# Passage to attention: the third unit's Q and K requested behind the first relayout, squares ahead of copies, and the halves of the first load run one after the other

## The chip, the cores and the metric

One core of one Trainium2 chip runs the whole kernel. The metric is device time in microseconds (us) for one execution, and the number compared is the median of several executions. The core's engines are named as in its profile: PE is TensorE (matrix multiply; PEld are its weight loads), DVE is VectorE, ACT is ScalarE, POOL is GpSimd and SP is SyncE, which here only issues DMA transfers. Each engine executes its own instructions strictly in program order; engines wait for each other, and for DMA transfers, by semaphores.

## What is computed

A linear recurrence in the style of attention, followed by two mixture-of-experts layers. Only the first part is touched by the change:

```python
mag = np.sqrt(a_re * a_re + a_im * a_im)
scale = np.minimum(mag, 0.999) / (mag + 1e-06)
a_re_n, a_im_n = (a_re * scale, a_im * scale)
for t in range(S):                       # S = 768, per batch (4), head (8), D = 48
    S_re, S_im = a[t] * (S_re, S_im)     # complex product, row by row
    S_re += k[:, :, t] (outer) v[:, :, t]
    y[:, :, t] = q[:, :, t] @ S_re
x = moe(y); x = moe2(x)                  # 3072 tokens, 8 experts each
```

The output is the result of the second expert layer, 3072 x 384 floats.

## The kernel before

The time axis is cut into chunks of 128 steps, 24 chunks over the 4 batches; two neighbouring chunks of a batch make a *unit*, 12 units in all. Three stages follow each other.

**The scan** (`prefix`). For all chunks at once the running products P of the normalized decays are formed, from the middle of a chunk outwards, 63 steps of two DVE instructions each: `t` (line 404, the four partial products) and `P` (line 409, their sums). The decays arrive as 16 loads `raw` of 8 steps (line 212, 215, requested by SP), and each load has two *halves* of 4 rows, so each half feeds two steps of the scan. Before a half can feed the scan, its magnitude is worked out: squares, their sum `u`, `mg` = exp(ln/2), `r` = 1/(mg + eps), `L` = r squared, `Aa`. For loads 2 to 15 this is `approx`, mostly on ACT with sums by PE into PSUM. For loads 0 and 1, when nothing else has begun, it is `approx_half`, with the sums on DVE; before the change the two halves of a load run in lockstep (`approx_halves`: every instruction comes twice, once for each half). A DVE routine `norm(j)` (five instructions) then makes the normalized decays `n` of half j, and ACT copies a negated part (line 340). The order in which all these stand is set by generators that are advanced by hand between the steps of the scan: `pull` advances the norms, `HV`, `AH`, `H0` and `H1` say how far the others go.

**The passage**. Behind the scan, the first units are prepared: `prod(n)` turns P and the loaded Q and K of unit n (tile `xy`, line 497; buffers for two units) into the tile `X`. It begins with two `squares` of P on ACT (line 542), an instruction on DVE (line 567), two on ACT (lines 568, 569), and then DVE products (line 565) and corrections (lines 575, 577, 579). When `X` of a unit is complete, `relayout` moves six pieces of it across partitions by DMA, three requested by POOL and three by SP (line 518), and `stack` makes a further copy `qst` (line 526). Units 0 and 1 are prepared completely before the attention loop; `chunk_ends` meanwhile makes the decay over a whole chunk with PE (`e_ps`), copies it on ACT (`e_sb`, line 456), writes it to DRAM (`pd`, line 457) and reads it back broadcast (`pb`, line 509).

**The attention loop**, 24 iterations, one chunk each: `scores` (PE, line 632), `masks` (DVE, line 636, product `sm` with the triangle), `kv`, `decay` (DVE, lines 673 to 677), `rows`, `store`. Between them DVE takes the pieces of `prod` for the unit two ahead. `scores(i + 1)` writes two PSUM tiles, which it can have once `masks(i)` has read them. The unit after the next is requested by `loads`: unit 2 and unit 3 ahead of the loop, the others inside it.

These lines of the passage are the ones that the change and the prediction speak of:

```python
        emit(first)                 # last pieces of prod(0), then relayout(0)
        loads_pb(0, nc.sync)
        ...
        emit(fill)                  # last pieces of prod(1), then relayout(1)
        loads(2)                    # POOL: Q and K of unit 2
        stack(U[0], SP)
        loads_pb(1, nc.sync)
        stack(U[1], SP)
        loads(3, nc.sync)           # SP: Q and K of unit 3
        scores(0, range(3, 4))
```

Of the kernel before, what the change touches and what calls it, by code (L numbers as in the profile page):

```python
# [9 lines left out]
F32 = mybir.dt.float32  # L10
# [3 lines left out]
ALU = mybir.AluOpType  # L14
# [16 lines left out]
G = B * (S // C) * 3  # L31
# [20 lines left out]
EARLY_FAST = 19  # L52
W0,W1,W2=(4, 5, 16)
LB,LA=(2, 1)
H0,H1=(6, 2)
HV=2
AH = 2
LEAD = 3
KP, SP = (3, 4, 5), ()
# [33 lines left out]
def emit(g):  # L93
    if g is not None:
        for _ in g:
            pass
# [89 lines left out]
def prefix(nc, tc, k, extra):  # L186
# [8 lines left out]
    with ExitStack() as c1:  # L195
# [55 lines left out]

        def buffers():
            return [wp.tile([128, 2, H, G], F32, name=nm, tag=nm, bufs=b)
                    for nm, b in (("mg", 1), ("L", 3), ("r0", 3), ("Aa", 3))]

        def rest(mg, L, r0, Aa):
            nc.scalar.activation(out=L, in_=mg, func=AF.Ln, bias=k.eps[:, 0:1])
# [7 lines left out]

        def approx(i):

            sq = wp.tile([128, 2, H, 2, G], F32, name="sq", tag="sq")
            nc.scalar.activation(out=sq.rearrange("p h t r g -> p (h t) r g"), in_=raw[i], func=AF.Square)  # L269
            mg, L, r0, Aa = buffers()  # L270
            yield

            def squares(x, last):
                for h in range(2):
                    for r in range(2):
                        nc.tensor.matmul(x[:, h, 0:n], k.idn, sq[:, h, :, r], start=r == 0, stop=last and r == 1)  # L276

            def view(x):
                return x[:, :, 0:n].rearrange("p h (t g) -> p h t g", g=G)

            m2 = mp.tile([128, 2, 512], F32, name="m2", tag="m2", bufs=1)
            squares(m2, True)
            for _ in range(2 if i < 4 else 4):
                yield
            nc.scalar.activation(out=L, in_=view(m2), func=AF.Ln, bias=k.tiny[:, 0:1])
            yield
            nc.scalar.activation(out=mg, in_=L, func=AF.Exp, scale=0.5)
            u = mp.tile([128, 2, 512], F32, name="u", tag="u", bufs=2)
            squares(u, False)
            for h in range(2):  # L290
                nc.tensor.matmul(u[:, h, 0:n], ide, mg[:, h], start=False, stop=True)
            pre[i] = view(u), L, r0, Aa
            yield
            yield
            yield from rest(mg, L, r0, Aa)

        def approx_half(i, h):

            if h == 0:
                u = mp.tile([128, 2, 512], F32, name="u", tag="u", bufs=2)  # L300
                sqs[i] = wp.tile([128, 2, H, 2, G], F32, name="sq", tag="sq")
                mgs[i], *lra = buffers()
                pre[i] = (u[:, :, 0:n].rearrange("p h (t g) -> p h t g", g=G), *lra)
            u, L, r0, Aa = (x[:, h] for x in pre[i])
            sq, mg = sqs[i][:, h], mgs[i][:, h]
            nc.scalar.activation(out=sq, in_=raw[i][:, h * H:h * H + H], func=AF.Square)
            yield
            nc.vector.tensor_tensor(u, sq[:, :, 0], sq[:, :, 1], op=ALU.add)
            nc.scalar.activation(out=L, in_=u, func=AF.Ln, bias=k.tiny[:, 0:1])
            yield  # L310
            nc.scalar.activation(out=mg, in_=L, func=AF.Exp, scale=0.5)
            yield
            nc.vector.scalar_tensor_tensor(out=u, in0=mg, scalar=2e-6, in1=u, op0=ALU.mult, op1=ALU.add)
            yield from rest(mg, L, r0, Aa)

        def approx_halves(i):
            for _ in zip(approx_half(i, 0), approx_half(i, 1)):
                yield

        def norm(j):  # L320

# [22 lines left out]

        load(0)
        load(1)
        firsts, halves = approx_halves(0), approx_halves(1)
        emit(islice(firsts, H0))
        emit(islice(halves, H1))
        emit(firsts)  # L350
        emit(norm(0))
        norms = chain(*(norm(j) for j in range(1, 2 * NP)))
        done = 0

# [6 lines left out]
        load(2)  # L361
        side = iter(())
        ahead = [approx(2)]
        load(3)
        routed = iter(())
        for i in range(NP):
# [10 lines left out]
            for h in range(2):  # L377
                j = 2 * i + h
                if h:
                    load(i + 4)  # L380
                    if i + 3 < NP:
                        ahead.append(approx(i + 3))
                cur = n3.pop(j)
                for ss in range(H2):
                    s = j * H2 + ss
                    a = cur[:, ss]
                    next(routed, None)
                    def more():
                        if s > 0:
                            for x in ahead:  # L390
                                for _ in range(AH):
                                    next(x, None)

                    if s == 0:
                        nc.vector.tensor_copy(P.a0, a[:, :, 0:G])
                        nc.vector.tensor_copy(P.t[:, 0, :, 1], a[:, 1:3, G:W])
                        more()
                        continue

                    if i == 0:  # L400
                        more()
                    t1 = tp.tile([128, 2, 2, W], F32, name="t1", tag="t1")
                    pairs = bass.AP(a.tensor, a.offset, [a.ap[0], [W, 2], [W, 2], [1, W]])
                    nc.vector.tensor_tensor(  # L404
                        t1, P.at(s - 1)[:, ::-1].unsqueeze(2).to_broadcast([128, 2, 2, W]), pairs, op=ALU.mult)
                    for _ in range(2 * HV):
                        next(halves, None)
                    pull(5 * j + min(LEAD, j) + (2 if ss == 0 else 4))
                    nc.vector.tensor_tensor(P.at(s), t1[:, 0], t1[:, 1], op=ALU.add)  # L409
                    pull(5 * j + min(LEAD, j) + (3 if ss == 0 else 5))  # L410
                    next(routed, None)
                    if ss:
                        next(side, None)
                    more()
        emit(side)


def chunk_ends(nc, k, psA, ep, wk):
# [35 lines left out]
    yield  # L454
    for par in range(2):
        nc.scalar.activation(out=e_sb[:, par], in_=e_ps[par].rearrange("n a r d -> n (a r d)"), func=AF.Copy)
    nc.sync.dma_start(out=k.pd, in_=e_sb)
    yield

    e2 = ep.tile([128, 2, 2 * G], F32, name="e2", bufs=1)  # L460
# [16 lines left out]
def attention(nc, tc, k, early, split):  # L477

    P = k.P
    with ExitStack() as c0:  # L480
# [123 lines left out]
        wk = c0.enter_context(tc.tile_pool(name="wk", bufs=2))  # L604
        lgb = psA.tile([128, 512], F32, name="lgb")
        wps = psA.tile([112, 4, 2, 48], F32, name="wps")
        nc.vector.memset(lgb[:, 0:128], 0.0)

        def ktr(i, rs):

# [139 lines left out]
        for _ in range(4):  # L750
            next(first)
            next(ends)
        emit(islice(first, FIRST - 4))
        next(ends)
        emit(islice(first, 4))
        squares(1, 1)
        emit(first)
        loads_pb(0, nc.sync)
        fill = prod(1, [(0, HC)])
        ktr(0, (0,))  # L760
# [18 lines left out]
        next(fill)  # L779
        ktr(0, (1,))  # L780
        emit(islice(fill, 2))
        kv(0)
        ktr(1, (0,))
        emit(fill)
        loads(2)
        stack(U[0], SP)
        loads_pb(1, nc.sync)
        stack(U[1], SP)
        loads(3, nc.sync)
        scores(0, range(3, 4))  # L790
        ktr(1, (1,))
        emit(masks(0))
        emit(decay(0))
        fill = iter(())
        for i in range(ni):
# [1276 lines left out]
```

## Time and profile before

| what | value |
|---|---|
| median of 3 runs | 694.84 us (692.77 to 696.39) |
| the profiled execution, its own time | 693.17 us |
| its span in the trace | 691.5 us |
| PE busy | 602.0 us, 87% |
| DVE busy | 567.3 us, 82% |
| ACT busy | 424.9 us, 61% |
| POOL busy | 214.9 us, 31% |

The span is what the trace shows from the first to the last instruction; the profiled execution took 1.7 us more than its span, and is itself 1.7 us quicker than the median of the runs. A busy share is an average over stages that have different limits, so what an edit is worth has to be read in its own stage. Times in the trace are counted from the start of the span.

### The profile page before, as it was taken

How to read it: one execution, taken by the hardware profiler on the slowest of the kernel's cores; microseconds unless marked ns; L12 is line 12 of the kernel's file. 1: busy time of each engine (PE TensorE's matmuls, PEld its weight loads, DVE VectorE, ACT ScalarE, POOL GpSimd, SP SyncE). 2: the span in 40 equal slices, each digit the busy share in tenths (PEclk: the TensorE clock that was granted, in tenths of full speed). 3: DMA queues.
4: the chain of work that ended last, by engine and by line, in shares of the span. 5: the costliest groups of instructions: out<-in, count | busy, mean ns of one | idle time of the engine just before them, and what ended most of it. 6: DMA issues, size and time to landing. Idle time of an engine off the chain costs nothing.

```text
span 691.5 us, 13765 instructions
## 1 busy us (share of the span) xinstructions
PE 602.0 (87%) x5024; PEld 524.1 (76%) x5024; DVE 567.3 (82%) x1218; ACT 424.9 (61%) x821; POOL 214.9 (31%) x300
## 2 busy tenths in 40 slices
PE   0799896327999999989988999999999998899996
PEld 0455564225788888878787999999999996678986
DVE  4999999986989989999799765666766677879993
ACT  6868886535457656553652655665655666478882
POOL 6400000001224332225344634444554452531101
PEclk9999999858899999999999999999999999999999
DMA  7889955006897889758350211551111168278840
GB/s 181 268 258 320 322 182 183 1 4 158 210 250 207 231 220 231 209 147 281 122 197 12 69 41 47 221 214 43 45 39 44 47 244 327 105 284 315 324 164 13
DMA packets 52167, 117.19 MB, mean 169 GB/s; under 512 B 11436, under 2 KB 40602, under 8 KB 47740
## 3 DMA queue, kind: packets, MB, share of 16 engines
q1 hardware_dynamic: 34524, 66.38, 30.9%
q0 software_dynamic: 14688, 45.94, 21.1%
q10 hardware_dynamic: 2880, 3.93, 1.8%
q8 instruction: 40, 0.66, 0.4%
q14 instruction: 35, 0.29, 0.1%
HBM read 116.84 MB, written 16.52 MB: 193 GB/s over the span
## 4 chain that ended last, share of the span: by engine, by line
PE 28%; DVE 9%; DMA 7%; issue 7%; ACT 2%; POOL 2%; POOLq 0%; ACTq 0%; DVEq 0%
PE yps L1522 11%; PE hps L1475 9%; DMA out_dram<-z,idx 3%; DMA out_dram<-y,idx 2%; DVE wlo L150 2%; DVE w L150 2%; PE gps L1351 1%; PE yps L1371 1%; DMA xg<-x,idx 1%; PE sc L632 1%; PE xtp L1459 1%; ACT w L149 1%; DVE hl L1482 1%; PE hps L1351 1%; PE yp L706 0%
## 5 line engine op out<-in xcount | busy, mean ns | idle before, releaser
L150 DVE TENSOR_TENSOR wlo<-wraw,whi 128x768 fp32r<-128x768 f32 (+1 forms) x95 | 82.3, 903 | 9.6 <-ACT whi L149 8.6
L150 DVE TENSOR_TENSOR w<-P,w 128x768 fp32r<-128x768 f32 (+1 forms) x95 | 82.6, 904 | 8.3 <-ACT w L149 7.1
L1482 DVE SCALAR_TENSOR_TENSOR hl<-hps,hh 128x512 fp32r<-128x512 f32 x48 | 33.1, 689 | 50.6 <-ACT hh L1481 47.6
L149 ACT ACTIVATE whi<-wraw 128x768 fp32r<-128x768 f32 (+1 forms) x95 | 71.0, 803 | 0.0
L149 ACT ACTIVATE w<-P 128x768 fp32r<-128x768 f32 (+1 forms) x95 | 70.8, 801 | 0.0
L1481 ACT ACTIVATE hh<-hps 128x512 fp32r<-128x512 f32 x48 | 28.7, 599 | 64.2 <-PE hps L1475 50.4
L276 PE MATMUL m<-sq,idn 128*128 128x288 f32 x112 | 35.6, 468 | 30.4 <-ACT sq L269 30.4
L1510 POOL DMA_INDIRECT out_dram<-y,idx x26 | 30.6, 1175 | 101.1 <-ACT y L1509 91.9
L632 PE MATMUL sc<-X 48*128 48x128 f32 x768 | 56.4, 293 | 5.0 <-DVE sm L636 4.5
L632 PEld LDWEIGHTS sc<-X 48*128 48x128 f32 x768 | 50.7, 201 | 10.2 <-DVE sm L636 5.2
L276 PEld LDWEIGHTS m<-sq,idn 128*128 128x128 f32 x112 | 22.7, 212 | 41.6 <-ACT sq L269 19.4
L518 POOL DMA_DIRECT2D X<-X x36 | 17.8, 502 | 107.4 <-DVE X L565 98.8
L1522 PE MATMUL yps<-w,hh 128*128 128x394 f32 x192 | 50.9, 346 | 0.0
L404 DVE TENSOR_TENSOR t<-P,n 128x576 f32<-128x576 f32 x63 | 47.5, 755 | 0.2
L1475 PE MATMUL hps<-xh,w 128*128 128x256 f32 x288 | 43.8, 282 | 3.4 <-DVE hl L1482 2.0
L1475 PEld LDWEIGHTS hps<-xh,w 128*128 128x128 f32 x288 | 38.1, 188 | 4.3 <-DVE hl L1482 2.4
L636 DVE TENSOR_TENSOR sm<-sc,tri 128x512 f32<-128x512 f32 x48 | 32.2, 684 | 8.4 <-PE sc L632 8.4
L436 POOL MEMSET ends<- 128x6 f32 x1 | 0.1, 105 | 121.6 <-DVE P L409 121.6
L704 PE MATMUL yp<-sm,v 128*64 128x128 f32 (+1 forms) x384 | 36.0, 275 | 0.0
L1522 PEld LDWEIGHTS yps<-w,hh 128*128 128x128 f32 x192 | 34.9, 189 | 0.0
L1522 PE MATMUL yps<-whi,hh 128*128 128x394 f32 x96 | 33.5, 349 | 0.0
L706 PE MATMUL yp<-qst,Ssb 96*48 96x128 f32 (+1 forms) x320 | 33.0, 282 | 0.0
(391 smaller groups left out, 1754.7 us busy)
## 6 DMA issues: line engine op xcount, KB each, us to landing
P<-in_w2t_dram SPq DMA_DIRECT2D x8, 1536.0 KB, 7.4
P<-in_v_dram SPq DMA_DIRECT2D x8, 1536.0 KB
wraw<-in_v_dram SPq DMA_DIRECT2D x8, 1536.0 KB, 7.5
qst<-X SPq DMA_DIRECT2D x48, 192.0 KB, 6.8
raw<-in_a_dram SPq DMA_DIRECT2D x32, 144.0 KB, 3.1
raw<-in_a_dram SPq DMA_DIRECT2D x64, 72.0 KB, 3.0
v<-in_v_dram POOLq DMA_DIRECT2D x12, 384.0 KB
out_dram<-xg SPq DMA_DIRECT2D x12, 384.0 KB, 3.7
```

The source lines that it names most:

```text
L149: self.nc.scalar.activation(out=hi, in_=r, func=AF.Copy)
L150: self.nc.vector.tensor_tensor(lo, r, hi.bitcast(F32), op=ALU.subtract)
L276: nc.tensor.matmul(x[:, h, 0:n], k.idn, sq[:, h, :, r], start=r == 0, stop=last and r == 1)
L404: nc.vector.tensor_tensor(t1, P.at(s - 1)[:, ::-1].unsqueeze(2).to_broadcast([128, 2, 2, W]), pairs, op=ALU.mult)
L632: nc.tensor.matmul(ps[:, pair], kk, q, start=r == 0, stop=r == 1)
L636: nc.vector.tensor_tensor(X[i].sm[:, 4 * g:4 * g + 4], X[i].sc[g], k.mask.to_broadcast([128, 4, 128]), op=ALU.mult)
L704: nc.tensor.matmul(o, U[n].v[:, c, h * 48:h * 48 + M], x.sm[:, 4 * par + pair], start=zero, stop=True)
L706: nc.tensor.matmul(o, x.sb[:, pair, 64 * par:64 * par + M], U[n].qst[:, h, cs], start=True, stop=False)
L1475: nc.tensor.matmul(ps[:, i], self.W.w1(s, wp_, j)[:, f * 128:f * 128 + 128], x[xp_][:, j], start=n == 0, stop=n == 8)
L1482: nc.vector.scalar_tensor_tensor(out=hl, in0=ps, scalar=0.0, in1=hh.bitcast(F32), op0=ALU.max, op1=ALU.subtract)
L1510: nc.gpsimd.indirect_dma_start(out=k.out, out_offset=IDX(ap=R.idx[:, c:c + 1], axis=0), in_=y, in_offset=None, bounds_check=N - 1, oob_is_ ...
L1522: nc.tensor.matmul(ps, hs[kk // 2][hp][:, kk % 2, us], self.W.w2(s, wp_, kk, Weights.DW), start=n == 0, stop=n == 23)
```

## The change

Six edits, in the scan's first load, in the passage, and in one table.

1. `loads(2)` is called behind `emit(first)`, so POOL issues the Q and K requests of unit 2 behind its part of `relayout(0)` and no longer behind that of `relayout(1)`.
2. `squares(1, 1)` comes ahead of the two `e_sb` copies on ACT, and the write `pd` is requested by ACT and no longer by SP.
3. `scores(0, range(3, 4))` (the fourth pair of heads, which reads what `relayout(0)` moved) stands ahead of `kv(0)` on PE.
4. The zeroing of `lgb` moves from the start of the passage to behind `masks(0)`.
5. The halves of load 0 run one after the other. For load 0 DVE takes over the second half's squares, and for both halves `L` = r squared and `Aa`, which ACT did. The tile `mg` has two buffers and `sq` three.
6. The halves of load 1 and the first pieces of `approx(2)` are advanced by a table `HV` for the first five steps. From the sixth step on, the order is the one of before.

```diff
-H0,H1=(6, 2)
-HV=2
+HV=(((), ()), ((1,), (3,)), ((3, 2), (2, 1)), ((4,), (0, 3, 1)), ((0, 2, 1), (0, 0, 2)))
...
-            nc.scalar.activation(out=sq, in_=raw[i][:, h * H:h * H + H], func=AF.Square)
+            r = raw[i][:, h * H:h * H + H]
+            if i == 0 and h == 1:
+                nc.vector.tensor_tensor(sq, r, r, op=ALU.mult)
+            else:
+                nc.scalar.activation(out=sq, in_=r, func=AF.Square)
...
+            nc.vector.tensor_tensor(L, r0, r0, op=ALU.mult)
+            yield
+            nc.vector.tensor_scalar(Aa, r0, -1e-6, 1.0, op0=ALU.mult, op1=ALU.add)
...
-        firsts, halves = approx_halves(0), approx_halves(1)
-        emit(islice(firsts, H0))
-        emit(islice(halves, H1))
-        emit(firsts)
-        emit(norm(0))
+        a0, a1 = approx_half(0, 0), approx_half(0, 1)
+        halves = chain(approx_half(1, 0), approx_half(1, 1))
+        w0 = norm(0)
+        for g, m in ((a0, 2), (a1, 1), (a0, 3), (a1, 2), (a0, 2), (a1, 1), (w0, 1), (a1, 1), (w0, 1), (a1, 1), (halves, 1),
+                     (w0, 9), (a1, 9)):
+            emit(islice(g, m))
...
         ahead = [approx(2)]
+        emit(islice(ahead[0], 2))
...
-    nc.sync.dma_start(out=k.pd, in_=e_sb)
+    nc.scalar.dma_start(out=k.pd, in_=e_sb)
...
-        nc.vector.memset(lgb[:, 0:128], 0.0)
...
-        emit(islice(first, FIRST - 4))
+        emit(islice(first, FIRST))
+        squares(1, 1)
         next(ends)
-        emit(islice(first, 4))
-        squares(1, 1)
         emit(first)
+        loads(2)
         loads_pb(0, nc.sync)
...
         emit(islice(fill, 2))
+        scores(0, range(3, 4))
         kv(0)
         ktr(1, (0,))
         emit(fill)
-        loads(2)
         stack(U[0], SP)
...
-        scores(0, range(3, 4))
         ktr(1, (1,))
         emit(masks(0))
+        nc.vector.memset(lgb[:, 0:128], 0.0)
```

What the edits make of the order, at three places. POOL in the passage, before (`X<-X` are pieces of a relayout, three for each unit; `xy` is the Q and K tile):

```order
L436 MEMSET ends 128x2x3
L518 DMA X<-X 16x1024 x6
L497 DMA xy<-in_q_dram 128x2x384
L497 DMA xy<-in_k_dram 128x2x384
L518 DMA X<-X 16x1024 x3
```

And of the change:

```order
L442 MEMSET ends 128x2x3
L524 DMA X<-X 16x1024 x3
L503 DMA xy<-in_q_dram 128x2x384
L503 DMA xy<-in_k_dram 128x2x384
L524 DMA X<-X 16x1024 x6
```

The two requests for unit 2 now stand between the relayouts of units 0 and 1. ACT at the end of `prod(0)`, before (`D` are the squares and their reciprocals, numbered by buffer; `kt` is a transposed K):

```order
L568 ACTIVATE D_911<-D_908 128x2x48
L569 ACTIVATE D_911<-D_911 128x2x48
L456 ACTIVATE e_sb<-e_ps_1355 24x384
L456 ACTIVATE e_sb<-e_ps_1356 24x384
L542 ACTIVATE D_1401<-P 128x384 x2
L620 ACTIVATE kt<-ktp 128x384
L568 ACTIVATE D_1401<-D_1338 128x768
L569 ACTIVATE D_1401<-D_1401 128x768
```

And of the change:

```order
L574 ACTIVATE D_911<-D_908 128x2x48
L575 ACTIVATE D_911<-D_911 128x2x48
L548 ACTIVATE D_1397<-P 128x384 x2
L462 ACTIVATE e_sb<-e_ps_1354 24x384
L462 ACTIVATE e_sb<-e_ps_1355 24x384
L463 DMA pd<-e_sb 48x1x384
L625 ACTIVATE kt<-ktp 128x384
L574 ACTIVATE D_1397<-D_1337 128x768
L575 ACTIVATE D_1397<-D_1397 128x768
```

The squares `D<-P` moved ahead of the copies, and a DMA request came in ahead of the next `kt` copy. DVE at the start, from the first sum `u` to the first step `t` of the scan, before:

```order
L308 TENSOR_TENSOR u<-sq 128x288 x2
L313 SCALAR_TENSOR_TENSOR u<-mg,u 128x288 x2
L308 TENSOR_TENSOR u<-sq 128x288 x2
L325 TENSOR_TENSOR L<-u,L 128x288
L327 SCALAR_TENSOR_TENSOR L<-L,r_224 128x288
L329 SCALAR_TENSOR_TENSOR L<-L,Aa 128x288
L339 TENSOR_TENSOR n_259<-raw,L 128x2x2x72
L342 TENSOR_TENSOR n_259<-raw,L 128x2x2x72
L395 COPY P<-n_259 128x216
L396 COPY P<-n_259 128x2x72
L404 TENSOR_TENSOR t_291<-P,n_259 128x576
```

And of the change, the last twelve rows up to the same step (five stand ahead of them: `u`, the second half's squares `sq`, `u` with `mg`, the second half's `u`, and the first half's `L`):

```order
L326 TENSOR_SCALAR Aa<-r_224 128x288
L316 SCALAR_TENSOR_TENSOR u<-mg,u 128x288
L334 TENSOR_TENSOR L<-u,L 128x288
L336 SCALAR_TENSOR_TENSOR L<-L,r_224 128x288
L324 TENSOR_TENSOR L<-r_224 128x288
L338 SCALAR_TENSOR_TENSOR L<-L,Aa 128x288
L348 TENSOR_TENSOR n_253<-raw,L 128x2x2x72
L351 TENSOR_TENSOR n_253<-raw,L 128x2x2x72
L326 TENSOR_SCALAR Aa<-r_224 128x288
L404 COPY P<-n_253 128x216
L405 COPY P<-n_253 128x2x72
L410 TENSOR_TENSOR t_286<-P,n_253 128x576
```

Ahead of the first step stands no work of load 1 any more (the second `u<-sq` pair of before), but five instructions came to DVE that ACT did.

## Rows read from the trace of the kernel before

**Rows 1.** Busy time by stretch: us, busy us (instructions) by engine, clock, DMA share, GB/s.

```profile
4.28:15.77 11.49, 0.00 (x0) 0.00 (x0) 5.43 (x13) 8.90 (x20) 7.32 (x29) 1.00 0.85 184
15.77:30.89 15.12, 12.78 (x40) 8.85 (x40) 13.94 (x29) 12.99 (x26) 7.01 (x11) 1.00 0.79 292
30.89:147.00 116.11, 80.27 (x448) 51.71 (x448) 115.90 (x269) 79.21 (x142) 0.00 (x0) 0.91 0.61 195
154.00:160.50 6.50, 4.84 (x58) 3.92 (x57) 5.37 (x8) 4.19 (x9) 1.48 (x3) 0.99 0.54 127
160.50:163.40 2.90, 0.44 (x3) 0.25 (x3) 2.87 (x7) 1.79 (x5) 0.36 (x1) 1.00 0.00 1
163.40:171.20 7.80, 7.70 (x61) 6.42 (x63) 3.76 (x7) 3.51 (x6) 2.58 (x5) 0.56 0.82 203
...
174.46:181.20 6.74, 6.74 (x51) 5.45 (x53) 6.71 (x13) 2.50 (x7) 0.00 (x0) 0.51 0.97 226
...
203.00:303.00 100.00, 98.13 (x1386) 84.77 (x1384) 91.69 (x181) 62.95 (x148) 32.38 (x58) 1.00 0.83 216
```

**Rows 2.** Timeline of the start: us from the start, us long, engine, line [idle before].

```profile
4.99 0.47 DVE L308 TENSOR_TENSOR u<-sq 128x288 f32<-128x288 f32 x1 [2.50 <-ACT sq L306]
...
5.74 0.68 ACT L306 ACTIVATE sq<-raw 128x576 f32<-128x576 f32 x1 [0.78 <-DMA raw<-in_a_dram]
...
9.26 0.77 ACT L259 ACTIVATE r<-L 128x288 f32<-128x288 f32 x2
...
15.77 0.76 DVE L404 TENSOR_TENSOR t<-P,n 128x576 f32<-128x576 f32 x1
...
30.89 0.75 DVE L404 TENSOR_TENSOR t<-P,n 128x576 f32<-128x576 f32 x1
```

**Rows 3.** Timeline of the passage, from the end of prod(0) to the first decay.

```profile
152.53 0.26 DVE L577 SCALAR_TENSOR_TENSOR D<-D,D 128x96 f32<-128x96 f32 x1
...
153.24 0.96 ACT L456 ACTIVATE e_sb<-e_ps 24x384 f32<-24x384 f32 x2 [1.03 <-PE e_ps L452]
...
154.10 0.92 ACT L542 ACTIVATE D<-P 128x384 f32<-128x384 f32 x2
...
154.22 1.00 SPq L457 DMA_DIRECT2D pd<-e_sb  x1
...
154.93 0.46 ACT L620 ACTIVATE kt<-ktp 128x384 f32<-128x384 f32 x1
...
155.06 0.96 DVE L567 SCALAR_TENSOR_TENSOR D<-D,D 128x768 f32<-128x768 f32 x1 [1.37 <-ACT D L542]
...
156.93 0.84 ACT L569 ACTIVATE D<-D 128x768 f32<-128x768 f32 x1
...
157.81 0.95 DVE L575 SCALAR_TENSOR_TENSOR D<-D,D 128x768 f32<-128x768 f32 x1
...
163.87 0.55 DVE L673 TENSOR_TENSOR St<-wps,pb 112x384 f32<-112x384 f32 x1
...
181.83 0.39 ACTq L742 DMA_DIRECT2D x<-xo  x1
```

**Rows 4.** Timeline around the wait for unit 2's Q and K, four engines.

```profile
153.98 1.50 POOL L518 DMA_DIRECT2D X<-X  x3 [6.60 <-DVE X L565]
...
165.24 0.74 POOL L497 DMA_DIRECT2D xy<-in_k_dram  x1
...
172.78 1.03 DVE L565 TENSOR_TENSOR X<-xy,P 128x384 f32<-128x384 f32 x2 [4.97 <-DMA xy<-in_k_dram]
...
174.46 3.66 PE L632 MATMUL sc<-X 48*128 48x128 f32 x30 [2.03 <-DVE sm L636]
...
175.81 0.58 SPq L497 DMA_DIRECT2D xy<-in_k_dram  x1
...
179.45 0.68 DVE L636 TENSOR_TENSOR sm<-sc,tri 128x512 f32<-128x512 f32 x1
...
184.45 1.02 DVE L565 TENSOR_TENSOR X<-xy,P 128x384 f32<-128x384 f32 x2
```

More of the change, by code (lines that the diff above doesn't have):

```diff
@@ L253, in buffers @@
             return [wp.tile([128, 2, H, G], F32, name=nm, tag=nm, bufs=b)
-                    for nm, b in (("mg", 1), ("L", 3), ("r0", 3), ("Aa", 3))]
+                    for nm, b in (("mg", 2), ("L", 3), ("r0", 3), ("Aa", 3))]
         def rest(mg, L, r0, Aa):
@@ L266, in approx @@
         def approx(i):
-            sq = wp.tile([128, 2, H, 2, G], F32, name="sq", tag="sq")
+            sq = wp.tile([128, 2, H, 2, G], F32, name="sq", tag="sq", bufs=3)
             nc.scalar.activation(out=sq.rearrange("p h t r g -> p (h t) r g"), in_=raw[i], func=AF.Square)
@@ L300, in approx_half @@
                 u = mp.tile([128, 2, 512], F32, name="u", tag="u", bufs=2)
-                sqs[i] = wp.tile([128, 2, H, 2, G], F32, name="sq", tag="sq")
+                sqs[i] = wp.tile([128, 2, H, 2, G], F32, name="sq", tag="sq", bufs=3)
                 mgs[i], *lra = buffers()
@@ L313, in approx_half @@
             nc.vector.scalar_tensor_tensor(out=u, in0=mg, scalar=2e-6, in1=u, op0=ALU.mult, op1=ALU.add)
[L314 to L318, printed above, removed]
+            if i > 0:
+                yield from rest(mg, L, r0, Aa)
+                return
+            nc.scalar.activation(out=L, in_=mg, func=AF.Ln, bias=k.eps[:, 0:1])
+            yield
+            nc.scalar.activation(out=r0, in_=L, func=AF.Exp, scale=-1.0)
+            yield
+            nc.vector.tensor_tensor(L, r0, r0, op=ALU.mult)
+            yield
+            nc.vector.tensor_scalar(Aa, r0, -1e-6, 1.0, op0=ALU.mult, op1=ALU.add)
+            yield
         def norm(j):
@@ L387, in prefix, with more @@
                     next(routed, None)
[L388 to L392, printed above, removed]
+                    def more(g):
+                        for x, m in zip((halves, *ahead), HV[s][g]) if s < len(HV) else ((x, g * AH) for x in ahead):
+                            emit(islice(x, m))
                     if s == 0:
@@ L396, in prefix @@
                         nc.vector.tensor_copy(P.t[:, 0, :, 1], a[:, 1:3, G:W])
-                        more()
                         continue
-                    if i == 0:
-                        more()
                     t1 = tp.tile([128, 2, 2, W], F32, name="t1", tag="t1")
@@ L405, in prefix @@
                         t1, P.at(s - 1)[:, ::-1].unsqueeze(2).to_broadcast([128, 2, 2, W]), pairs, op=ALU.mult)
-                    for _ in range(2 * HV):
-                        next(halves, None)
-                    pull(5 * j + min(LEAD, j) + (2 if ss == 0 else 4))
+                    goal = 5 * j + min(LEAD, j) + 3 * ss
+                    more(0)
+                    pull(goal + (1 if ss else 2))
                     nc.vector.tensor_tensor(P.at(s), t1[:, 0], t1[:, 1], op=ALU.add)
-                    pull(5 * j + min(LEAD, j) + (3 if ss == 0 else 5))
+                    pull(goal + (2 if ss else 3))
                     next(routed, None)
@@ L413, in prefix @@
                         next(side, None)
-                    more()
+                    more(1)
         emit(side)
```

## Prediction

> **What bounds the kernel now.** I read the busy time by stretch first, then the timelines of the two places that the edits touch. DVE is the limit of the scan: from 30.89 to 147 us it is busy 115.90 of 116.11 us, while ACT and PE have gaps [rows 1]. So whatever brings the scan's first steps forward is kept as long as ACT, PE and the loads keep up, and the place to look for it is the start, where DVE is busy only 5.43 of 11.49 us before its first step [rows 1]. Behind 203 us PE is the limit (98.13 of 100 us [rows 1]), and what is won ahead of the loop shifts the loop as a whole, since everything in it is released by its own chain. Between the two lies the passage, and its timeline shows one hole that stands out: from 172.78 - 4.97 = 167.81 on DVE waits for Q and K of unit 2 [rows 4]. K was requested by POOL at 165.24, behind the second relayout, so from request to use it took 172.78 - 165.24 = 7.5 us [rows 4]. A smaller hole is at 155.06, where DVE waits 1.37 us for squares that ACT begins at 154.10 [rows 3].
>
> **The early request.** POOL's part of the first relayout is issued from 153.98 on and takes 1.50 us [rows 4]; the two requests follow it at 155.5 and 156.3. Their buffer is that of unit 0, whose reads end within a microsecond of line 577 at 152.53 [rows 3], so nothing holds them. With the slow 7.5 us of before, K lands at 163.8. DVE wants it at 167.8 by the old clock of the passage. The 4.97 us are therefore gone, with 4 us to spare.
>
> What is late next? DVE's first mask behind the hole, at 179.45, needs PE's scores, and becomes due at 174.4. PE had begun these scores, stopped at 172.4 (174.46 - 2.03) because the second mask of the iteration before had not freed its tile, and did the other 30 pieces in 3.66 us, in a stretch with a granted clock of 0.51 [rows 4, 1]. Without the hole the tile is free by about 169.5, PE doesn't stop, and ends at 172.4 + 3.66 = 176.1 at half clock, or at 174.2 at full clock. PE had been busy 7.70 of 7.80 us up to 171.2, at 0.56 on the mean, so near half clock with a rise towards the end [rows 1]; I take full clock, no new wait, and -5.0. The bounds are -3.3 (half clock, 1.7 us of waiting) and -5.0: more can't come of it, since DVE is busy 6.71 of the 6.74 us up to 181.2 [rows 1].
>
> The transfer now shares the DMA engines with the relayout of unit 0 and with the way of the chunk ends through DRAM (`pd`, then `pb`). That stretch has a DMA share of 0.54, and from 160.5 to 163.4 DMA does nothing at all [rows 1], so `pb` had landed by 160.5, and DVE first needs it at 163.87 [rows 3]: 3.4 us of room. The transfer of 768 KB takes 3.9 us at the 203 GB/s of the next stretch [rows 1]; if `pd` and `pb` stood still for all of it, DVE would wait 0.5 us. I take 0, bound +0.5.
>
> By the Trainium skill ("DMA: Bandwidth & Descriptors", section on queues, rings and completion order) a DMA engine takes turns between the queue rows that have work, a packet at a time; then `pd` and `pb` would lose about half of that time and the bound would be 0.
>
> PE meets the relayout too: the fourth pair's scores now stand ahead of `kv(0)` and wait for it, and behind them ACT's `kt` copies. The relayout had landed by 160.5 as well, and DVE's masks, two products of 0.6 each ahead of 163.87, are due at 162.6. I take 0, and come back to it under the rivals.
>
> **Squares ahead of copies.** The squares need a tile that DVE last reads at 152.53 + 0.26, so they can stand from 152.85 to 153.8, in the 1.03 us that ACT idles ahead of `e_sb` [rows 3]. Line 567 then starts when DVE is free, at 155.06 - 1.37 + 0.15 = 153.85. But the next DVE row that depends on ACT, line 575 at 157.81, stands behind ACT's own queue: `e_sb` to 153.8 + 0.96 = 154.76, the new DMA request, the `kt` copy (0.46), and lines 568 and 569 (0.84 each, with 0.1 of handing over), in sum 157.0 plus the request [rows 3]. A request on ACT occupies 0.39 us in the loop; this one occupied 1.00 us on SP [rows 3]. So line 575 comes at 157.4 to 158.0, -0.4 to +0.2 us, and I take -0.1, nearer to the row of the same transfer. SP, relieved, issues its part of the relayout some 1 us earlier, which nothing waits for. The zeroing of `lgb` is one short instruction on DVE's path before and after: 0.
>
> **The start.** The first half's sum `u` is done at 4.99 + 0.47 = 5.46 [rows 2]. From there the first half had to share ACT with the second: each instruction came twice, and load 1's squares before the first step. In the new order I give a row that waits for the one ahead 0.49 us (0.47 and a little handing over), and one that doesn't 0.38 (half of the 0.77 of two halves [rows 2]). ACT: logarithm, exponential, logarithm, exponential, to 7.46. DVE meanwhile: the second half's squares from 5.74, when its data are there, to 6.5 (0.76, as the equally large row of line 404 [rows 2]); `u` with `mg` to 7.0; the second `u` to 7.46; `L` to 7.9, `Aa` to 8.3. ACT goes through its four for the second half, `mg` at 8.47; DVE adds it, to 9.0. Then norm 0, with the second half's `L` in between, to 11.5; `Aa`, two copies, and the first step at 12.3 instead of 15.77: 3.4 us earlier. Walked on in the same way, DVE waits for ACT's rows of load 1 at 16.1 (`mg`), 17.6 (`L`), 21.3 and 23.2 (the same of its second half), and the sixth step stands at 28.1 instead of 30.89 [rows 2]: -2.8. From there the order is that of before, and DVE is saturated. I take off 0.5 for unit 3: its PE sums begin at about 26, behind a gap in PE's work, and if they run at half clock its `L` is ready at 34.9 against a need at 34.3. So -2.3.
>
> The bounds: DVE's idle time up to 30.89 is 6.06 + 1.18 = 7.2 us [rows 1], from which the five new DVE instructions take 2.3 (0.76, and four of 0.38), so no more than -4.9; and 0, if ACT's chain for the later loads gives all of it back.
>
> **The sum.** -5.0 - 0.1 - 2.3 = -7.4 us. Against the profiled execution's own 693.17 that is 685.8; that execution is 1.7 us below the median of the runs, 694.84, from which it would be 687.4. I forecast 686.5. A difference of 0.5%, 3.5 us, is about what a measurement of this kernel can tell from no change.
>
> **The rivals.**
>
> *The next request takes the place of the removed one.* K of unit 3 is requested by SP at 175.81 and used at 184.45, which becomes 179.4 [rows 4]. From 163.4 to 181.2 DMA is busy 0.82 to 0.97 [rows 1], so this transfer lands near 181; if it still did, DVE would wait 1.6 us, and if it took 7.5 us from the end of an unmoved request, 4.5 us. Against it: 768 KB of that traffic, 3.9 us, move out of the stretch, and SP's requests come behind those transfers. The sum would be -5.8 to -2.9: 687.4 to 690.3.
>
> *The start is given back.* If ACT's chain or the loads hold the later steps, DVE gets waits of 2.3 us between 31 and 147 us, and the passage alone remains: -5.1, 688.1. For it: ACT is busy 12.99 of 15.12 us up to 30.89 [rows 1]. Against it: DVE takes over about 2.2 us of that.
>
> *Both, or as much in other waits:* 690.3 plus 2.3, so 690 to 693.
>
> *The clock's gift.* PE works from 174.46 to 181.2 at 0.51 [rows 1], after 2.03 us of idleness [rows 4]. At full clock the same work takes 3.4 us less, and if PE held that stretch the sum would be -10.8: 682.4. Against it: DVE is busy in all of that stretch [rows 1]. The Trainium skill ("TensorE: Matmul & The Clock Gate", Part 1) has the clock follow how busy the engine has lately been, so that a wait is paid a second time in slow matmuls; by that the removed hole returns more than its own length.
>
> *Slower.* PE's fourth-pair scores wait for the relayout, now with 768 KB beside it. If it lands at time L, 8 pieces of scores (8 x 0.122 us, from 3.66 for 30 [rows 4]) bring DVE's masks to L + 1.0, due at 162.6. The gain of 7.4 is used up at L = 169.0, and the kernel is slower by over 0.5% from 172.5 on. The relayout is requested from 153.98 on, so this needs 17 us and more, where the K of unit 2 took 7.5 [rows 4].
>
> **How the numbers follow.** The forecast has 0.55 (own range 683.5 to 689.0); the next request 0.10, the start given back 0.12, the clock's gift 0.05, all faster by over 0.5% (under 691.4); both or as much 0.13, within 0.5%; slower 0.05. Faster 0.82, same 0.13, slower 0.05. For 8 in 10 the range runs from 682.0 (the start at its bound, or the clock's gift) to 692.0, which leaves out the slower case and a part of the one of both.
>
> **What would show it.** The first step `t` at about 12.3, the sixth near 28.1, and no more than 1 us of DVE waits from there to the end of the scan; POOL's two requests right behind its three relayout pieces; no wait for `xy` at the product behind the mask; on ACT a DMA request of 0.4 to 1.0 us ahead of the `kt` copy; PE's scores of iteration 2 without a stop. The forecast is wrong if DVE waits for `xy` of unit 3 or for `pb`, if ACT's rows of loads 2 to 4 come late, or if PE is not ready when DVE is.

## The result and the profile after

The changed kernel takes 685.68 us (median of 4 runs, 685.30 to 686.71) against 693.81 for the kernel before on the same chips: ratio 0.9881, interval 0.9845 to 0.9916. Its profiled execution took 686.71 with a span of 685.0, 6.5 less than before. Busy time by stretch (columns as in [rows 1]). The first three stretches are cut where the prediction had the first and the sixth step, 12.3 and 28.1; they stand at 12.39 and 28.96:

```profile
4.28:12.30 8.02, 0.00 (x0) 0.00 (x0) 6.67 (x16) 6.03 (x12) 7.02 (x28) 1.00 0.77 202
12.30:28.10 15.80, 10.44 (x23) 6.88 (x24) 14.12 (x30) 12.17 (x24) 7.22 (x12) 0.80 0.79 253
28.10:144.30 116.20, 86.50 (x467) 56.23 (x465) 115.43 (x268) 81.75 (x147) 0.00 (x0) 0.91 0.60 202
...
157.50:163.40 5.90, 5.04 (x34) 3.88 (x36) 5.49 (x10) 1.95 (x5) 1.37 (x3) 0.50 0.52 157
163.40:168.00 4.60, 4.60 (x42) 4.07 (x41) 3.53 (x7) 1.93 (x5) 0.13 (x1) 0.50 0.80 194
168.00:175.00 7.00, 6.98 (x98) 5.88 (x96) 6.96 (x14) 4.15 (x9) 0.00 (x0) 0.95 1.09 249
```

DVE is nearly as saturated in the scan (third row) as before: idle for 0.77 of 116.20 us, most of it one wait of 0.63 for ACT, against 0.21 of 116.11 [rows 1]. The passage now runs at half clock up to 168 and at nearly full clock from there. Before, it was the other way round: full up to 163.4, then 0.56 to 171.2 and 0.51 from 174.46 to 181.2 [rows 1]. This differs between executions too: in a second profile of the changed kernel (run 9 below) the clock was 1.00 from 154.0 to 156.4 and 0.50 from 158.9 to 171. What DVE waits for between 150 and 200 us has changed its names: the 5.0 us for `xy` are gone, and a wait for `pb` is new.

```profile
DVE D L581 <- ACT D L575: 1.7, 2, 1.5
DVE St L678 <- DMA pb<-pd: 1.3, 1, 1.3
DVE sm L641 <- PE sc L637: 0.6, 1, 0.6
DVE D L573 <- ACT D L548: 0.2, 1, 0.2
```

The timeline of the start, several engines:

```profile
12.39 0.76 DVE L410 TENSOR_TENSOR t<-P,n 128x576 f32<-128x576 f32 x1
...
19.54 0.76 DVE L348 TENSOR_TENSOR n<-raw,L 128x288 f32<-128x288 f32 x1
19.95 0.72 POOL L1755 TENSOR_TENSOR lbw<-mf,bi 128x192 f32<-128x192 f32 x1
20.22 0.77 DVE L311 TENSOR_TENSOR u<-sq 128x288 f32<-128x288 f32 x1
20.75 0.68 POOL L1757 TENSOR_TENSOR lb<-lb,lbw 128x192 f32<-128x192 f32 x1
20.91 1.14 DVE L410 TENSOR_TENSOR t<-P,n 128x576 f32<-128x576 f32 x1
...
26.78 4.21 PE L275 MATMUL m<-sq,idn 128*128 128x288 f32 x8 [1.86 <-ACT sq L268]
...
28.96 0.75 DVE L410 TENSOR_TENSOR t<-P,n 128x576 f32<-128x576 f32 x1
...
35.85 0.46 DVE L334 TENSOR_TENSOR L<-u,L 128x288 f32<-128x288 f32 x1 [0.63 <-ACT L L260]
```

The first step stands at 12.39 instead of 15.77 [rows 2], the sixth at 28.96 instead of 30.89. From the ninth step to the last every `t` is 1.22 us earlier than before. Three more rows of DVE that the account below uses, two of the kernel before and one of the change:

```profile
167.12 0.69 DVE L636 TENSOR_TENSOR sm<-sc,tri 128x512 f32<-128x512 f32 x1 [0.58 <-PE sc L632]
...
201.20 0.69 DVE L636 TENSOR_TENSOR sm<-sc,tri 128x512 f32<-128x512 f32 x1 [0.79 <-PE sc L632]
```

```profile
195.28 0.69 DVE L641 TENSOR_TENSOR sm<-sc,tri 128x512 f32<-128x512 f32 x1 [0.62 <-PE sc L637]
```

The timeline of the passage:

```profile
152.32 1.91 SPq L524 DMA_DIRECT2D X<-X  x3
...
152.47 0.96 DVE L573 SCALAR_TENSOR_TENSOR D<-D,D 128x768 f32<-128x768 f32 x1 [0.17 <-ACT D L548]
...
153.21 1.40 ACTq L463 DMA_DIRECT2D pd<-e_sb  x1
...
154.83 0.74 POOL L503 DMA_DIRECT2D xy<-in_k_dram  x1
...
156.78 0.96 DVE L581 SCALAR_TENSOR_TENSOR D<-D,D 128x768 f32<-128x768 f32 x1 [1.48 <-ACT D L575]
...
157.47 1.32 SPq L515 DMA_DIRECT2D pb<-pd  x2
157.72 1.32 PE L637 MATMUL sc<-X 48*128 48x128 f32 x8 [0.88 <-DMA X<-X]
...
164.40 0.56 DVE L678 TENSOR_TENSOR St<-wps,pb 112x384 f32<-112x384 f32 x1 [1.28 <-DMA pb<-pd]
...
167.00 0.68 DVE L641 TENSOR_TENSOR sm<-sc,tri 128x512 f32<-128x512 f32 x1
167.60 1.02 DVE L571 TENSOR_TENSOR X<-xy,P 128x384 f32<-128x384 f32 x2
...
170.49 2.16 PE L637 MATMUL sc<-X 48*128 48x128 f32 x32
```

Set against [rows 3, 4], DVE's lead on the kernel before reads: 1.38 us ahead of the passage (1.22 from the start, 0.16 from the zeroing of `lgb`, which moved behind the masks), 2.59 at the first row behind the squares (152.47 against 155.06), 1.03 behind the request on ACT (156.78 against 157.81), minus 0.53 behind the zeroing and the wait for `pb` (164.40 against 163.87), 0.12 at the next mask, 5.18 at the product with unit 2's Q and K (167.60 against 172.78). It is 5.24 at 190, 5.91 from 195 to 300, and 6.5 at the end. The last 0.6 arise behind 325 us, where the two kernels are equal; what they come from was not looked into.

### The profile page after: what moved, and what is told of

Its sections match the earlier page's. It is cut to its first block, busy times and chain, and to the rows that moved or that the text cites. A ratio compares the mean times of both kernels' runs of the same rounds, so it can differ in the third digit from the quotient of the medians.

```text
span 685.0 us, 13757 instructions
## 1 busy us (share of the span) xinstructions
PE 605.5 (88%) x5024; PEld 526.5 (77%) x5024; DVE 569.5 (83%) x1223; ACT 423.5 (62%) x816; POOL 213.0 (31%) x300
## 4 chain that ended last, share of the span: by engine, by line
PE 26%; issue 12%; DMA 8%; DVE 5%; POOL 3%; ACT 1%; POOLq 0%; ACTq 0%; DVEq 0%
PE yps L1527 10%; PE hps L1480 8%; DMA out_dram<-z,idx 5%; DMA out_dram<-y,idx 2%; PE yps L1376 1%; PE hps L1356 1%; DMA xg<-x,idx 1%; DVE wlo L149 1%; PE sc L637 1%; POOL xq L1798 1%; PE xtp L1464 1%; POOL wraw L123 1%; DVE hl L1487 1%; DMA xq<-out_dram,idx 1%; POOL P L123 0%
## 5 line engine op out<-in xcount | busy, mean ns | idle before, releaser
L275 PE MATMUL m<-sq,idn 128*128 128x288 f32 x112 | 37.4, 486 | 25.2 <-ACT sq L268 25.2
L1449 POOL DMA_INDIRECT xg<-x,idx x24 | 28.1, 1173 | 16.6 <-issue 11.8
```

## The experiments

All use the comparison with the kernel before on the same chip. For each profile two lengths are read: when the last of the scan's 63 `t` starts (before: 145.82), and how long it takes from there to the eighth row of L573 (before L567, at 210.06), in the loop; I call the second the passage.

| kernel | last `t` | passage | ratio to before, interval |
|---|---|---|---|
| before | 145.82 | 64.24 | 1 |
| changed | 144.60 | 59.55 | 0.9881, 0.9845 to 0.9916 |
| changed, again | 144.88 | 60.37 | 0.9878, 0.9829 to 0.9928 |
| 1 early request alone | 145.67 | 59.64 | 0.9924, 0.9896 to 0.9951 |
| 2 start alone | 144.85 | 64.09 | 0.9980, 0.9956 to 1.0004 |
| 3 pd on SP | 144.62 | 61.22 | 0.9935, 0.9908 to 0.9961 |
| 4 Q, K behind pb | 144.68 | 59.06 | 0.9861, 0.9830 to 0.9892 |
| 5 both | 143.52 | 58.78 | 0.9864, 0.9826 to 0.9901 |
| 6 matmuls ahead of the passage | 143.91 | 66.94 | 1.0033, 1.0006 to 1.0060 |
| 7 request at the old place | 144.22 | 67.15 | 1.0027, 0.9994 to 1.0061 |
| 8 as 5, with 6 | 144.08 | 65.11 | 1.0008, 0.9979 to 1.0036 |
| 10 as 5, hole filled | 143.88 | 59.12 | 0.9856, 0.9808 to 0.9904 |
| 11 holes at the start filled | 144.06 | 59.21 | 0.9870, 0.9822 to 0.9918 |
| 12 as 10, with 11 | 144.40 | 56.87 | 0.9842, 0.9793 to 0.9891 |

Each row has one profile. The two profiles of the changed kernel differ by 0.8 us in the passage, so smaller differences there say nothing. Of the totals, only those of 2, 6, 7 and 8 can be told from the change's; the intervals of the others overlap with its own.

**1. The early request alone** (on the kernel before):

```
         emit(first)
+        loads(2)
         loads_pb(0, nc.sync)
...
-        loads(2)
         stack(U[0], SP)
```

> The kernel before with one edit: the two requests for unit 2's Q and K stand right behind POOL's part of the first relayout. First theory (the gain of 6.5 us of span is 1.2 from the start, and 5.1 from this request, and the wait for pb behind the first masks comes from sharing the DMA engines with it): DVE's 4.97 us wait for xy is gone, a wait of 0.5 to 1.5 us for pb stands ahead of L673's first instruction though pd is on SP as before, most of it gives back the 0.58 us wait for scores, and the kernel is 4.5 to 5.7 us faster than the kernel before (some 688.5). Rival (pb is late in the changed kernel because its source pd is written by a request on ACT): no wait for pb here. Rival (the start carries most of the gain): under 4 us faster.

The passage is 4.6 us shorter, the ratio 0.76% below 1, some 5.3 us. The wait for `pb` of the first theory isn't there; DVE waits for the fourth pair's scores instead, since PE waits for the relayout:

```profile
162.10 1.31 PE L632 MATMUL sc<-X 48*128 48x128 f32 x8 [2.59 <-DMA X<-X]
...
163.33 1.29 DVE L636 TENSOR_TENSOR sm<-sc,tri 128x512 f32<-128x512 f32 x2 [0.73 <-PE sc L632]
```

So the size was as the first theory had it, but the wait beside it was another one: SP requests its relayout pieces at 155.17, behind `pd`, and they share the DMA engines with Q and K.

**2. The start alone:** the changed kernel with the whole passage of before, the place of the fourth pair's scores and of the zeroing of `lgb` included.

```
-        emit(islice(first, FIRST))
-        squares(1, 1)
+        emit(islice(first, FIRST - 4))
         next(ends)
+        emit(islice(first, 4))
+        squares(1, 1)
         emit(first)
-        loads(2)
...
+        loads(2)
         stack(U[0], SP)
...
-    nc.scalar.dma_start(out=k.pd, in_=e_sb)
+    nc.sync.dma_start(out=k.pd, in_=e_sb)
```

> The changed kernel with the passage and the zeroing of lgb as before, so only the first load's halves, load 1's rows and the buffers are new. First theory: every step of the scan from the tenth on stands 1.2 us earlier than before, the passage follows with all its waits, 1.2 us faster (0.17%, less than can be told from no change by the total; the trace tells it). The prediction's term: 2.3 us. Rival (the start is worth nothing by itself, what it wins comes back as waits later in the scan): 0.

The last `t` is 0.97 us earlier and the passage as long as before (64.09). The first theory holds, in one execution (the same start brought between 0.94 and 2.30 us in the others); the total alone could not have told it from nothing.

**3. `pd` on SP:** the one line `nc.scalar.dma_start(out=k.pd, ...)` as `nc.sync.dma_start`.

> The changed kernel with the write of the chunk ends to DRAM (pd) requested by SP again, ahead of its part of the first relayout; the squares stay ahead of the copies. First theory (the 1.40 us that this request takes on ACT is DVE's 1.48 us wait for the reciprocals): that wait falls to 0.1 us and the first masks start at 160.2 instead of 161.65; pb, which lands beside unit 2's Q and K, is then waited for longer, 1.5 to 2.7 us, so that 0 to 1 us of the 1.4 is left. Rival (pb is late because of the request on ACT): the wait for pb goes too, and the gain over the changed kernel is 1.5 to 2.5 us.

Both theories missed. DVE's wait for the reciprocals is gone, as expected, but the passage is 0.9 to 1.7 us longer than that of the two profiles of the change:

```profile
154.32 1.88 SPq L524 DMA_DIRECT2D X<-X  x3
...
161.69 1.32 PE L637 MATMUL sc<-X 48*128 48x128 f32 x8 [4.83 <-DMA X<-X]
...
162.92 1.29 DVE L641 TENSOR_TENSOR sm<-sc,tri 128x512 f32<-128x512 f32 x2 [2.65 <-PE sc L637]
```

SP's relayout pieces, 2.0 us later, land beside Q and K, 5.5 us behind the end of their requests; in the changed kernel PE goes on at 157.72, 3.5 us behind it.

**4. Q and K behind `pb`:**

```
         emit(first)
-        loads(2)
         loads_pb(0, nc.sync)
+        loads(2, nc.sync)
```

> The changed kernel with unit 2's Q and K requested by SP right behind the two requests for pb instead of by POOL ahead of them. First theory (pb is late because the transfer of Q and K is under way beside it): the wait of 1.28 us for pb is gone, the masks of the next iteration then wait for PE's scores, so 0.3 to 0.7 us are won by iteration 2, provided that K, requested at about 159, is there at 167; a wait for xy stays under 0.5 us. Rival (pb is late for another reason, the request on ACT): the wait for pb stays at about 1.3 us.

The wait for `pb` is gone, K is there in time though requested 4.8 us later, and PE's scores, at half clock for most of their 3.90 us, are the next limit. `pd` is still requested by ACT here, so that request is not what made `pb` late:

```profile
159.67 0.61 SPq L503 DMA_DIRECT2D xy<-in_k_dram  x1
...
163.11 0.53 DVE L678 TENSOR_TENSOR St<-wps,pb 112x384 f32<-112x384 f32 x1
...
165.99 0.69 DVE L641 TENSOR_TENSOR sm<-sc,tri 128x512 f32<-128x512 f32 x1 [0.23 <-PE sc L637]
```

**5. Both edits, 3 and 4.**

> The changed kernel with both edits of the two runs before: pd requested by SP ahead of its relayout pieces, and unit 2's Q and K by SP behind pb. Theory as revised by those runs (what counts in the passage is what shares the DMA engines with the first relayout and with pb; the request on ACT pays only because it lets SP's relayout pieces go ahead of Q and K): with Q and K behind both, the relayout lands at 157 to 158.5, the fourth pair's scores cost nothing, DVE's wait for the reciprocals is 0.1, the first masks start at 160.2, no wait for pb, the next masks at 164.5 to 165 (limited by PE's scores at half clock); iteration 2 stands 1.0 to 1.4 us earlier than with Q and K behind pb alone and 2.0 to 2.4 earlier than in the changed kernel: 683 to 684. Rival (pd on SP makes the relayout late by itself, because its pieces are requested 1.9 us later): PE's fourth-pair scores wait past 160 and the gain is gone.

The relayout is there at 157.14 with `pd` on SP too, so its lateness in 3 was Q and K's doing; DVE waits nowhere for K, though it is requested 2.8 us later than in the change. DVE's masks start at 159.09, nothing waits for `pb`, and the wait has gone to the next scores:

```profile
157.14 0.83 PE L637 MATMUL sc<-X 48*128 48x128 f32 x8 [2.88 <-DMA X<-X]
...
161.04 3.79 PE L637 MATMUL sc<-X 48*128 48x128 f32 x32
...
164.85 0.69 DVE L641 TENSOR_TENSOR sm<-sc,tri 128x512 f32<-128x512 f32 x1 [1.72 <-PE sc L637]
```

**6 and 8. Extra matmuls in the last nine steps,** on the changed kernel (6) and on 5 (8):

```
                     pull(goal + (2 if ss else 3))
+                    if s >= HC - 9:
+                        for _ in range(6):
+                            nc.tensor.matmul(wps[:, 0:288], k.idn, P.at(s - 1), start=True, stop=True)
```

> The changed kernel with extra matmuls on PE, six in each of the last nine steps of the scan, into a bank that nothing reads afterwards, so that PE isn't idle for 19 us ahead of the passage. Theory: the granted clock from 151 to 168 us is near 1 instead of 0.50, the scores, kt transposes and state sums of the passage take half the time, but DVE is released there by ACT and by pb, not by PE: iteration 2 stands within 0.3 us of the changed kernel's, and 0 to 0.7 us are won by 195 us, where PE is the limit. Rival (the half clock of the passage holds it, through kt, the state sums and the copies behind them): more than 1.5 us earlier at iteration 2.

> The changed kernel with pd on SP, unit 2's Q and K on SP behind pb, and the extra matmuls in the last nine steps of the scan. Theory: as with pd and the requests alone, and the masks of the next iteration no longer wait for scores at half clock: they start at 164.2 to 164.5; K of unit 2, requested at about 158, is wanted at 165 and may be waited for by up to 1 us; 0 to 0.7 us better than without the extra matmuls, 682 to 683.5.

Both failed as tests. In the trace each of these matmuls is two instructions of 0.25 us, so six take 3 us, more than a step lasts. PE ran behind, and the chunk ends came 6.7 us late (lines of run 6):

```profile
147.67 8.17 PE L419 MATMUL wps<-P,idn 128*128 128x288 f32 x33
155.94 1.99 PE L461 MATMUL e_ps<-idn,ends 128*24 128x48 f32 x48
...
162.11 0.96 DVE L584 SCALAR_TENSOR_TENSOR D<-D,D 128x768 f32<-128x768 f32 x1 [7.49 <-ACT D L578]
```

In the changed kernel `e_ps` begins at 149.26. The two runs show one thing: whatever delays `e_sb` on ACT delays DVE's reciprocals with it, since ACT keeps its order.

**7. The request at its old place,** all else as changed:

```
         emit(first)
-        loads(2)
         loads_pb(0, nc.sync)
...
         emit(fill)
+        loads(2)
         stack(U[0], SP)
```

> The changed kernel with unit 2's Q and K requested at their old place, behind the second relayout. Theory: DVE waits 4.5 to 6 us for xy ahead of the second mask of the next iteration; pb isn't waited for; the fourth pair's scores start without a wait at about 157; the loop stands 4.0 to 5.2 us later than in the changed kernel. Rival (the early request only moves the wait): under 2.5 us.

The passage is 6.8 to 7.6 us longer than in the changed kernel, more than the 4.0 to 5.2 expected, and 2.9 longer than before the change:

```profile
163.83 0.74 POOL L503 DMA_DIRECT2D xy<-in_k_dram  x1
...
173.12 1.03 DVE L571 TENSOR_TENSOR X<-xy,P 128x384 f32<-128x384 f32 x2 [6.21 <-DMA xy<-in_k_dram]
...
174.81 3.78 PE L637 MATMUL sc<-X 48*128 48x128 f32 x30 [3.40 <-DVE sm L641]
```

K is requested 1.4 us earlier than before [rows 4] and used 9.3 us after it instead of 7.5; why it took longer isn't shown. PE stops for longer, and its scores run at half clock behind it.

**The changed kernel again (9), and matmuls into holes (10 to 12).** The fill of the passage (10) on 5, the fill of the start (11) on the changed kernel, both on 5 (12):

```
+        for _ in range(8):
+            nc.tensor.matmul(lgb[:, 136:424], k.idn, P.at(HC - 1), start=True, stop=True)
         scores(0, range(3, 4))
...
             squares(u, False)
+            if i == 2:
+                for _ in range(8):
+                    nc.tensor.matmul(wps[:, 0:288], k.idn, sq[:, 0, :, 0], start=True, stop=True)
...
+            if i == 2:
+                for _ in range(8):
+                    nc.tensor.matmul(wps[:, 0:288], k.idn, sq[:, 0, :, 0], start=True, stop=True)
             pre[i] = view(u), L, r0, Aa
```

> The changed kernel itself, once more, as the comparison for the three below and for how far one execution's start differs from another's. In the runs so far the scan of kernels with the new start ended 0.97 to 2.30 us earlier than in the kernel before, with the PE sums of loads 2 and 3 at about half clock each time. Expected: scan end at 143.5 to 144.9, the wait for pb of 0.5 to 1.5 us again, 685 to 687.

The scan ended where expected (144.88). The wait for `pb`, 2.11 us, was longer than the 0.5 to 1.5 written down, and the time, 688.31 (683.39 to 689.63), above the 685 to 687:

```profile
165.51 0.56 DVE L678 TENSOR_TENSOR St<-wps,pb 112x384 f32<-112x384 f32 x1 [2.11 <-DMA pb<-pd]
```

> The kernel with pd on SP and unit 2's Q and K on SP behind pb, and eight extra matmuls on PE (into a part of a bank that is written anew later) in the hole in which PE waits for the relayout ahead of the fourth pair's scores. Theory (DVE's 1.72 us wait for the scores of the next iteration is PE at half clock, and the half clock is the price of that hole): the 32 score matmuls run in 2.2 us instead of 3.8, the wait falls under 0.3 us, and iteration 2 stands 0.8 to 1.7 us earlier against the scan's end than without the extra matmuls, unless K of unit 2 (wanted at 164) is late. Rival (the clock does not depend on that hole): nothing, or up to 0.3 us later for the extra work.

> The changed kernel with eight extra matmuls on PE behind load 2's sums and eight behind its last ones, in the two holes of PE at 20 to 22.6 and 24 to 26.7 us. Theory (the 0.63 us wait at the ninth step is load 3's sums at half clock): the sums of load 3 run in 2.2 and 2.1 us, that wait is gone, and the scan ends 0.6 to 0.8 us earlier than in the changed kernel; the sixth step is where it was. Rival (load 3's rows on ACT are late by themselves): the wait stays.

> Both sets of extra matmuls, pd on SP and unit 2's Q and K on SP behind pb. Theory: the sum of the parts, 2.0 to 3.5 us below the changed kernel: 681 to 684. Rival: the places won run into the next limit, PE's work from 165 us on, and under 1.5 us are left.

Eight matmuls are 16 instructions in the trace, so each fill took 4.0 to 4.5 us, more than the hole in the passage (2.88 in run 5). In 10 the fill began at half clock and held the fourth pair's scores up to 160.36, so that DVE's masks waited 1.60 us; but from there the clock stayed at 1.00, the 32 scores took 2.16 us and DVE's wait for them was 0.15; the passage is no shorter than that of 5. In 12 the fill ran at full clock, and nothing was held up:

```profile
154.65 4.05 PE L794 MATMUL lgb<-P,idn 128*128 128x288 f32 x16
158.62 0.74 PE L643 MATMUL sc<-X 48*128 48x128 f32 x8
...
161.93 2.16 PE L643 MATMUL sc<-X 48*128 48x128 f32 x32
...
164.12 0.69 DVE L647 TENSOR_TENSOR sm<-sc,tri 128x512 f32<-128x512 f32 x1 [0.15 <-PE sc L643]
```

Its passage is 1.9 us shorter than that of 5 and 2.7 to 3.5 shorter than that of the change. So the wait of 1.72 us in 5 is PE at half clock. That the half clock follows PE's hole rests on two executions, 5 and 12, with full clock ahead of the hole in both. The level there isn't set by the program alone: 10 has the program of 5 up to the hole, and its clock was 0.50 from 152 to 156.4, where that of 5 was 0.98 to 1.00. In 11 load 3's sums ran at full clock (2.10 each) but began at 28.34 instead of 26.78, behind the fill, and the wait of 0.63 stayed: ACT goes on behind them 0.54 us earlier than in the changed kernel (30.48 against 31.02), and DVE comes there 0.54 earlier too. Run 11 thus decides nothing on what the half clock costs here, but other profiles do: where these sums took 4.21 us (the changed kernel and 3, 8, 10) the wait was 0.63, where 4.07 to 4.11 (2, 7, 9) 0.50 to 0.53, where 3.98 (6) 0.40, where 3.83 (4) 0.25, and where 3.68 (5) there was none. The wait shrinks as much as the sums do. 12 has the lowest ratio, 0.9842 (684.52 us, where 681 to 684 was expected): a gain over the change is shown in the trace of the passage, not in the total.

## Why the prediction was right

The forecast of 686.5 and its mechanism, the early request as the largest part, held. That it came within 1 us is partly luck: the smaller terms missed by 1.5 us together, 0.6 us came where nothing was forecast, and the same kernel, measured again in run 9, took 688.31. The terms, against the profiled execution:

- *The early request, -5.0:* the lead grows by 5.06 between the next mask and the product behind it, and PE's scores of iteration 2 ran without a stop at full clock (2.16 us). Run 1, with it alone, gives 4.6 in the passage. Run 7 shows that its worth depends on the rest: without it the other edits would make the passage 2.9 us longer. The rival of the next request is out: SP requests K of unit 3 at 171.78 instead of 175.81, and DVE waits for no `xy` up to 200 us.
- *pb, 0 with a bound of 0.5:* the step "3.4 us of room" failed. The room itself was smaller, 2.7 us: before the change the two transfers for `pb` landed at 160.79 and 161.20, not by 160.5. `pb` was requested at 157.47 as before, but used at 164.40, after a wait of 1.28 us (2.11 in the second profile, none in run 11, which has the same order in the passage). It never was waited for where Q and K came behind it (runs 4, 5, 10, 12). Each of the two lands in 16 shares, and the trace has an event for each. Of the second one's, 15 had landed by 162.20 (163.05 in the second profile), 0.9 to 1.4 us later than before the change, and ahead of DVE's need at 163.12 (163.40). The Trainium skill ("DMA: Bandwidth & Descriptors", section on queues, rings and completion order) has each DMA engine take turns between its queue rows, a packet at a time. The trace agrees for these 15, whose delay is under half of the 3.9 us of Q and K. The wait is the last share alone, at 164.28 (165.38), for which the prediction has no term. Ahead of it ran a single packet of another queue, 16 KB of instructions, from 161.89 to 162.90 (161.86 to 163.09), and within 0.02 us of its end the remaining packets for `pb` begin. The view of the DMA queues from 161.8 to 163.0 us has it:

```profile
q8 instruction: 1, 0.02, 5.2%
```

  In run 11 that packet ran from 158.65 to 159.53, and the last share landed by 161.89. In runs 4 and 7 a last share is late behind it too, but DVE came later still. The traces don't name the engine of a packet, so that this packet held the share up is read from the times. By this reading the early Q and K moved the tail of `pb` to where the packet ran, and an execution waits if the two meet.

  Of the 1.28, 0.58 were had back at once: the wait for scores of 167.12 before fell away.
- *Squares ahead of copies, -0.1:* with the request it became +0.35, above the upper bound of +0.2. The squares won 1.21 us, as worked out (155.06 to 153.85); the request on ACT took 1.40 us instead of 0.4 to 1.0 and gave 1.56 back. The zeroing is 0 as said: 0.16 won ahead of the squares and 0.17 lost behind the masks.
- *SP's earlier relayout pieces, "which nothing waits for":* wrong, and the prediction's main miss in mechanism. With `pd` on SP (runs 1 and 3) PE's fourth pair waits 2.59 and 4.83 us for the relayout. This is the rival called slower, at L = 162.1 and 161.7, against the 169.0 from which it would have used up the gain. The request on ACT costs 1.56 us on DVE and buys the relayout its place ahead of Q and K.
- *The start, -2.3:* it brought 1.22 (0.94 in the second profile, 0.97 in run 2, 2.30 in run 5; all twelve profiles with the new start lie between these). The first step came as walked (12.39 for 12.3), and the loss at load 3 (the prediction's "unit 3"), taken as 0.5, was 0.71 from the sixth step to the tenth. The walk failed in between: it priced DVE's rows as if alone. Beside POOL's rows at 19.4 to 21.4 us three of them took 0.76, 0.77 and 1.14 instead of 0.46, 0.46 and 0.76, in sum 1.0 us, about what the sixth step is late (28.96 for 28.1). The trace of before showed it, beside the same work of POOL:

```profile
20.09 0.77 DVE L342 TENSOR_TENSOR n<-raw,L 128x288 f32<-128x288 f32 x1
20.96 0.97 DVE L404 TENSOR_TENSOR t<-P,n 128x576 f32<-128x576 f32 x1
```

- *The clock's gift:* priced at -3.4 with PE holding that stretch, it came as -0.7, at 195 us, where PE's lead (its scores at 185.89 against 192.04, 6.15 us) passed to DVE, whose lead had been 5.24. That PE's lead comes from the clock is argued from the two traces; no run isolates it.

In sum -1.2 + 0.35 + 1.4 - 0.65 - 5.1 - 0.7 = -5.9 by 195 us, against -7.4 in the prediction; with the 0.6 behind 325 us, -6.5. The start was too hopeful by 1.1 us and the squares with the request by 0.45, the waits that came and went around `pb` cost 0.75, and the clock gave 0.7.

## What to carry to other kernels

A transfer that is requested early takes its place among those already due: ask which smaller ones it will share the engines with, and put it behind those that are waited for first, as far as its own need allows (run 5 requested K 2.8 us later than the change did and still had it in time). An edit's worth is read with the others in place: here the same request was worth 4.6 us alone and about 7 with the rest, in the passage. In a walk through an engine's rows, price those beside another engine's work by rows that stood beside such work. Where a transfer has room to spare, look whether its last share has it too: here 15 of 16 were in time.

## What was not expected of the hardware

- DVE rows with two inputs took 0.3 to 0.4 us longer while POOL's elementwise rows ran (0.77 for 0.46, 1.14 for 0.76). That is a reason for the shortfall at the start that the Trainium skill names: "SBUF — State Buffer", section on the two separate sides, gives DVE and GpSimd a port pair that only one of them holds at a time. The trace agrees in direction.
- The start of one and the same program differs between executions: with the new start the last `t` stood between 143.52 and 144.88. One part follows POOL: its three rows at L1755 and L1757 wait for a load and began between 18.8 and 21.8 us. Where they began at 18.8 to 18.9 (runs 2, 4, 9), the sixth step stood at 29.33 to 29.43; at 19.4 (the changed kernel and 3) it stood at 28.96 to 28.99; at 20.2 and later (5, 6, 8, 10 to 12), past some of the DVE rows that they had slowed, at 28.24 to 28.50. The other part is the wait at the ninth step, for load 3's sums.
- In run 5 PE's granted clock fell to half behind the 2.88 us in which PE was idle up to 157.14, and it stayed at full in run 12, where extra matmuls filled that hole. A fill that started at half clock cost as much as it won (run 10). Up to that hole 10 is the same program as 5, yet one came to it at half clock and the other at full.
- A 16 KB packet of instructions ran for 0.9 to 1.2 us among the data of the passage, from a start between 153.6 us (run 12) and 164.1 (run 3). It shows as a wait only where the tail of `pb` was still under way, in the changed kernel and run 9.
